# An attention-and-feed-forward kernel: seven products in place of eight in five output projections, and a planner with new costs

## The chip, the cores and the metric

The kernel runs on one core of a Trainium2 chip. The metric is the device time of one execution in microseconds (us). Before the change it is 1092.83 us, the median of three runs (1092.67 to 1093.36). A core has four engines that compute: PE (TensorE, matrix products), DVE (VectorE), ACT (ScalarE) and POOL (GpSimd). SP issues DMAs. Each engine works through its own instruction list in order and waits on semaphores for the others.

## The reference

Three stages follow each other, all in float32. Attention with a sigmoid in place of softmax, 4 batches, 12 heads, 448 positions, head size 64:

```python
scores = scale * np.matmul(q, k.transpose(0, 1, 3, 2)) - np.log(S)
attn = 1.0 / (1.0 + np.exp(-scores))
attn_out = np.matmul(attn, v)
```

Then a first feed-forward layer on the 1792 rows of width 768, and a second one with a gate:

```python
h = x @ w_in                          # 768 -> 2048
x = (h - np.tanh(h)) @ w_out          # 2048 -> 768
gate = 1.0 / (1.0 + np.exp(-(x @ w_gate)))   # 768 -> 1536
val = x @ w_val
out = (gate * val) @ w_out2           # 1536 -> 768
```

## The kernel before, in words

Products are made in float32 accuracy from operands that are split in two: a "high" part (ACT casts it) and a "low" part (DVE or POOL subtracts the high part). Each product is three matmuls, high by high, high by low and low by high, 448 columns wide. The four batches are the tiles t = 0 to 3.

*First layer.* For 32 steps i, `hidden_mm` computes a hidden block of 256 columns in 36 matmuls (`ph`, L399), ACT and DVE turn it into `g` by a chain of 12 operations (L433 to L472: squares, tanh, a polynomial, a predicated copy, then high and low of `g`), and a step of `po` matmuls (L506, 36 of them in six groups d = 0 to 5) projects it into `acc`. A group either adds `acc` on DVE (L519) or is seeded: ACT copies `acc` into the bank (L494), PE adds on top, ACT copies it back (L623). The last three steps are `tail_step`; the six groups of the very last step are put among the work of the second layer as "fillers".

*Second layer.* It runs in two passes over pairs of batches (`ps` 0 and 1), six blocks of 256 hidden columns each, so twelve blocks k = 0 to 11 (`block`, L1008). Both batches of a pair are multiplied together by seven products in place of eight (a 2 by 2 block scheme: operands `a11, a12, a22, s1 ... s4`, weights `b1, b22, t14, t32` mixed from four quarters). A product is nine matmuls (L1038). A block is seven products for the gate, n = 3k, and seven for the value, n = 3k+1, with the joins, copies and sigmoids between them, and ends with `gg`, high and low. The output projection of block k, n = 3k+2, stands in `groups2(k)`: for each of the two batches six groups of six matmuls (`pq`, L506), 72 in all. These groups are the fillers of block k+1: a plan `f{k}` of 14 numbers says how many groups stand behind each product.

*Operands.* `prepare` makes the x operands of a pass from `acc` (L667 sums, L801 high, L807 low). `divide` loads a block's 256 columns of weights (`mm`), mixes the quarters on DVE (L911, L916, L918), casts the high part on ACT (L881) and subtracts the low part on POOL or DVE (L892). Seven slots `w0` to `w6` hold them. `decoding` unpacks stored weights early (L181 to L199).

*What sets the order.* From step 28 of the first layer on, instructions are laid out by a planner in the kernel: `Task` objects with due times, `spend` which lets tasks start while PE works through a product, `must` for operations with a fixed place. It has a clock per engine (`busy`) and a clock `now` that follows PE's matmuls, with costs as constants in the code. Table `TUNE` shifts due times and chooses engines. The clock `now` grows by a fixed length per product:

```python
    def must(e, cost, f, ready=0.0):
        busy[e] = max(busy[e], now[0], ready) + cost
        f()
        return busy[e]
```

It does not stand still when PE must wait for a bank or an operand; only `force` moves it for an operation that has been left too late.

Of the kernel before, what the change touches and what calls it, by code (L numbers as in the profile page):

```python
# [64 lines left out]
}  # L65


@with_exitstack
def kernel(
# [462 lines left out]
    def groups1(i):  # L532

        at, gt, outs = outs1(i)
        for d in range(KD):
            def run(d=d):
# [4 lines left out]
                must("v", 0.65, lambda: sum_up(at, po, d, False, None))  # L541
# [66 lines left out]
    def tail_step(i, act, dve):  # L608
# [5 lines left out]
        def group(d):  # L614
            p = None
            if d % 2 and i > TAIL2:
                p = seeds.pop(d)
            p = project_group(f"po{i}_{d}", at, gt, outs, d, False, p, evict=False)
            if d % 2 == 0 and i > TAIL2:
                seeds[d + 1] = must("a", 0.55, lambda: None) and seed(f"po{i}_{d + 1}", at, d + 1)  # L620
            spend(1.2, TUNE.get("e4", 0.9), TUNE.get("e5", 1.0))
            if d % 2 and i > TAIL2:
                must("a", 0.55, lambda: nc.scalar.activation(  # L623
                    out=at[:, d], in_=p[:, :S], func=AF.Copy
                ))
# [12 lines left out]
        t4 = chain.add(dict(a=1.0), q2, [t2])
        td = chain.add(dict(v=1.1), d_, [t4])
# [42 lines left out]
    class Task:  # L682
# [11 lines left out]
        def start(self):  # L694
# [6 lines left out]
            if len(ways) > 1 and not self.haste and ways[1][0] < self.due - SPARE:  # L701
                return ways[1]
# [713 lines left out]
```

## Time and profile before

| | us |
|---|---|
| median of the runs | 1092.83 |
| the profiled execution | 1092.74 |
| its span (first to last instruction) | 1091.0 |
| PE busy in the span | 1078.5 (99%) |
| DVE, ACT, POOL busy | 822.6, 617.8, 384.9 |
| matmuls in the trace | 6085 |

The times of the rows come from the profiled execution; 1.74 us of it lie outside the span. A matmul here is a weight load that overlaps the matmul ahead, and the matmul itself. A mean duration of 362 ns in the page is that of one instruction in a pipeline; what a matmul takes out of the time is read from the chain of waits, which gives the start of each run of matmuls and their number. Line numbers are those of the kernel before.

### The profile page before, as it was taken

What the parts mean: (1) busy time and instruction counts of PE and PEld (TensorE: products, weight loads), DVE (VectorE), ACT (ScalarE), POOL (GpSimd) and SP (SyncE); (2) the same over time, 40 slices, a digit from 0 to 9 for tenths busy, and PEclk for the clock granted to TensorE, in tenths of its full rate; (3) what the DMA queues carried; (4) which work ended last, traced back from release to release, by engine and by line L of the source; (5) the groups of instructions that cost most, each with busy time, mean ns of one, the idle gap of its engine ahead of it and who ended that gap; (6) DMA issues with size and microseconds to landing.
All of it is one profiled execution on the core that took longest, in us unless ns stands there. A gap on an engine that the chain in (4) does not pass through costs nothing.

```text
span 1091.0 us, 15944 instructions
## 1 busy us (share of the span) xinstructions
PE 1078.5 (99%) x6085; PEld 971.6 (89%) x6085; DVE 822.6 (75%) x1153; ACT 617.8 (57%) x861; POOL 384.9 (35%) x391
## 2 busy tenths in 40 slices
PE   9999999999999999999999899999999999999998
PEld 5677789999999999999998799999999999999997
DVE  4778757899998989899978878898849664454344
ACT  6878845676777767777767545343454333333320
POOL 5455300011111110111126445565578524544621
PEclk9999999999999999999999999999999999999999
DMA  7676303334243434244320255454221411201202
GB/s 203 194 192 182 110 22 87 102 104 132 85 144 102 145 102 137 85 130 138 120 73 30 101 174 174 124 181 134 98 88 65 153 59 59 87 29 59 87 1 102
DMA packets 40204, 119.79 MB, mean 110 GB/s; under 512 B 6080, under 2 KB 21440, under 8 KB 40128
## 3 DMA queue, kind: packets, MB, share of 16 engines
q1 hardware_dynamic: 36896, 116.38, 33.2%
q0 software_dynamic: 3072, 2.17, 0.9%
q8 instruction: 48, 0.79, 0.3%
q10 hardware_dynamic: 160, 0.23, 0.1%
q14 instruction: 28, 0.23, 0.1%
HBM read 99.09 MB, written 19.66 MB: 109 GB/s over the span
## 4 chain that ended last, share of the span: by engine, by line
PE 96%; ACT 1%; DMA 1%; DVE 1%; POOL 0%; issue 0%; SPq 0%; ACTq 0%; DVEq 0%; POOLq 0%
PE ph L399 21%; PE po L506 21%; PE pq L506 16%; PE pa L1038 8%; PE pc L1038 8%; PE pb L1038 8%; PE pv L383 5%; PE pe L1038 4%; PE sa L346 4%; PE sl L358 1%; PE pv L376 1%; DMA st<-in_w_in_dram 0%; ACT at L350 0%; DMA kt<-in_k_dram 0%; POOL gg L1106 0%
## 5 line engine op out<-in xcount | busy, mean ns | idle before, releaser
L506 PE MATMUL po<-g,w 128*128 128x448 f32 x1152 | 238.9, 364 | 2.9 <-ACT g L469 2.7
L399 PE MATMUL ph<-x,w 128*128 128x448 f32 x1152 | 235.8, 362 | 0.2 <-ACT at L350 0.2
L506 PEld LDWEIGHTS po<-g,w 128*128 128x128 f32 x1152 | 215.2, 189 | 21.3 <-ACT g L469 3.0
L399 PEld LDWEIGHTS ph<-x,w 128*128 128x128 f32 x1152 | 215.8, 187 | 15.3 <-ACT at L350 0.6
L214 POOL TENSOR_TENSOR w<-m,w 128x384 fp32r<-128x384 f32 x64 | 63.6, 1016 | 376.5 <-issue 299.0
L506 PE MATMUL pq<-gg,w 128*128 128x448 f32 x864 | 184.3, 362 | 1.4 <-POOL gg L1106 0.8
L506 PEld LDWEIGHTS pq<-gg,w 128*128 128x128 f32 x864 | 161.8, 187 | 13.2 <-POOL gg L1106 1.5
L892 POOL TENSOR_TENSOR w_t<-mm,w_t 128x384 fp32r<-128x384 f32 x72 | 79.9, 1131 | 141.6 <-ACT w_t L881 137.8
L519 DVE TENSOR_TENSOR acco<-pq,acco 128x448 f32<-128x448 f32 x120 | 73.7, 621 | 72.9 <-PE pq L506 72.2
L1038 PE MATMUL pa<-a,w_b 128*128 128x448 f32 x432 | 94.2, 362 | 0.0
L1038 PEld LDWEIGHTS pa<-a,w_b 128*128 128x128 f32 x432 | 81.0, 187 | 5.4
L892 POOL TENSOR_TENSOR w_b<-mm,w_b 128x384 fp32r<-128x384 f32 x54 | 63.6, 1198 | 38.9 <-ACT w_b L881 36.7
L350 ACT ACTIVATE at<-sa,bias_s 128x896 f32<-128x896 f32 x72 | 67.3, 1006 | 8.1 <-PE sa L346 7.9
L436 ACT ACTIVATE y<-ph 128x896 f32<-128x896 f32 x32 | 29.4, 919 | 61.9 <-PE ph L399 61.9
L519 DVE TENSOR_TENSOR acc<-po,acc 128x448 f32<-128x448 f32 x90 | 55.4, 617 | 9.3 <-PE po L506 9.2
L181 ACT ACTIVATE m<-st 128x768 f32<-128x768 f32 x32 | 29.0, 907 | 56.6 <-POOL w L214 55.0
L383 PE MATMUL pv<-at,vt 128*64 128x224 f32 x576 | 59.8, 357 | 0.0
L383 PEld LDWEIGHTS pv<-at,vt 128*64 128x64 f32 x576 | 39.2, 137 | 18.9 <-issue 8.0
L346 PE MATMUL sa<-sp 64*128 64x448 f32 x432 | 50.8, 375 | 0.5 <-DVE sp L319 0.3
L1106 POOL TENSOR_TENSOR gg<-sg,gg 128x448 fp32r<-128x448 f32 x30 | 39.7, 1347 | 31.3 <-ACT gg L1101 31.1
L881 ACT ACTIVATE w_t<-mm 128x768 fp32r<-128x768 f32 x48 | 39.5, 838 | 19.9 <-DVE mm L918 14.1
L346 PEld LDWEIGHTS sa<-sp 64*128 64x128 f32 x432 | 38.5, 184 | 12.2 <-issue 7.3
(114 smaller groups left out, 1867.6 us busy)
## 6 DMA issues: line engine op xcount, KB each, us to landing
mm<-kept SPq DMA_DIRECT2D x36, 768.0 KB, 4.3
st<-in_w_out_dram SPq DMA_DIRECT2D x28, 768.0 KB, 4.9
st<-in_w_in_dram SPq DMA_DIRECT2D x16, 768.0 KB, 4.3
st<-in_w_gate_dram SPq DMA_DIRECT2D x12, 768.0 KB, 5.0
st<-in_w_val_dram SPq DMA_DIRECT2D x12, 768.0 KB, 4.9
kept<-mk SPq DMA_DIRECT2D x22, 384.0 KB, 5.5
kt<-in_k_dram SPq DMA_DIRECT2D x48, 112.0 KB, 3.5
kept<-mq SPq DMA_DIRECT2D x14, 384.0 KB, 5.6
```

The source lines that it names most:

```text
L214: (low or nc.gpsimd).tensor_tensor(out=w1[:, r], in0=mf[:, r], in1=w0[:, r].bitcast(F32), op=ALU.subtract)
L346: nc.tensor.matmul(pa[:, j, :S], kk[r, ki, c], qq[r, qi], start=(i == 0), stop=(i == 2),)
L350: nc.scalar.activation(out=at[:, :, c], in_=pa[:, :, :S], func=AF.Sigmoid, bias=bias_s, scale=qk_scale,)
L383: nc.tensor.matmul(po[j * D:(j + 1) * D, h, :SH], vt[:, j, c], at[:, j, c, h * SH:(h + 1) * SH], start=False, stop=(c == NCH - 2),)
L399: nc.tensor.matmul(o, w(i), xv(j), start=first and n == 0, stop=last and n == 2, skip_group_check=seeded,)
L436: nc.scalar.activation(out=y, in_=h, func=AF.Tanh)
L506: nc.tensor.matmul(po[:, :S], w[:, a, d], gt[:, c, j], start=n == 0 and not seeded, stop=n == last, skip_group_check=seeded,)
L519: nc.vector.tensor_tensor(out=at[:, d], in0=po[:, :S], in1=at[:, d], op=ALU.add)
L881: nc.scalar.activation(out=w0, in_=quarters(lo, hi), func=AF.Copy)
L892: eng.tensor_tensor(out=w1[:, r], in0=quarters(lo, hi)[:, r], in1=w0[:, r].bitcast(F32), op=ALU.subtract,)
L1038: nc.tensor.matmul(bank[term], w[:, i, half * KH + c], t[:, j, c], start=fresh and at == 0, stop=at == 3 * KH - 1, skip_group_check=not fresh,
L1106: eng.tensor_tensor(out=gt[t][:, 1, j], in0=sg[t][:, j], in1=gt[t][:, 0, j].bitcast(F32), op=ALU.subtract,)
```

## The change

In the second pass, five of the six output projections, those of blocks 6 to 10 (`wide(k)`), are computed by seven products in place of eight as well, now over both batches at once: 7 products by 3 column groups by 3 matmuls, 63 matmuls in place of 72. For this `divide` prepares the output weights of these blocks in the form that the other two matrices already have (four casts and four mixes in place of two casts, with an eighth slot and a half slot), `combine` mixes the block's result into the operands `t1` to `t4`, and `groups3` issues the products as eight fillers with their own banks (`a`, `b`, `c`, `e`), copies between banks on ACT, and 15 evictions on DVE in place of 12. What is common to both batches is gathered in a tile `accm`, and added once at the end (`shared`). Block 11 and the first pass keep `groups2`.

The planner gets new costs (smaller throughout), a clock `l` for operations of DVE and POOL that it holds to exclude each other, ready times for banks and operands (`until` moves `now` when PE is planned to wait), and a `lag` that due times are shifted by. All numbers of `TUNE` are new. The first block takes the product `a12` ahead of `s2` (`TERMS0`).

```diff
-    "f0": [0, 0, 4, 0, 0, 0, 2, 0, 0, 0, 0, 0, 0, 0],
+    "early": 3, "f0": [0, 0, 5, 0, 1, 0, 0, 0, 0, 0, 0, 0, 0, 0],
...
+    TERMS0 = ("a11", "s1", "a12", "s2", "s3", "s4", "a22")
...
     def must(e, cost, f, ready=0.0):
-        busy[e] = max(busy[e], now[0], ready) + cost
+        busy[e] = max(busy[e], now[0] + 0.2, ready) + cost
         f()
-        return busy[e]
+        return busy[e] + SHOW
+
+    def until(t, who=None):
+        if t > now[0]:
+            lag[0] += t - now[0]
+            now[0] = t
...
+            ways = []
+            for e, cost in kinds.items():
+                at = max(t, busy[e], busy["l"] if lock else 0.0)
+                ways.append((at + cost, at, e))
...
+    def wide(k):
+        return NBLK <= k < NK - 1
...
-        if kind == 2:
-            pair(0, 0, 2, [ld])
-            pair(1, 2, 4, [ld])
+        either = dict(v=0.485, g=0.93)
+        if wide(k) and kind == 2:
+            b22 = pair("b22", [3], [ld])
+            b1 = pair("b1", [0, 2], [ld])
+            t = task.add(either, mix(3, 1, 3, ALU.add), [b22])
+            t = task.add(either, mix(1, 0, 1, ALU.subtract), [t, b1])
+            pair("t14", [1, 3], [t])
+            t = task.add(either, mix(0, 3, 0, ALU.subtract), [t])
+            t = task.add(either, mix(2, 2, 0, ALU.subtract), [t])
+            pair("t32", [0, 2], [t])
...
+            operand("t1", 6.0, u1, lambda c: gt[1][:, c, 0], b12, b11)
+            operand("t2", 8.0, u2, lambda c: gt[2][:, 1, c], b22, u1, "t1")
+            operand("t3", 10.0, b12, lambda c: gt[2][:, 0, c], b22, b12, "t1")
+            operand("b22", 10.5, b22, lambda c: gt[1][:, c, 1])
+            operand("t4", 13.0, u4, lambda c: gt[2][:, 2, c], b21, u2, "t2")
...
+    PLAN_W = [0, 0, 1, 0] + [1] * 7 + [0] * 3
...
+        def pa_(d):
+            mm("p1", d, "a")
+            return lambda: copy("b", "a", d), 0.6
+
+        def pb_(d):
+            mm("p5", d, "e")
+            mm("p2", d, "a")
+            mm("p6", d, "b")
+
+            def then():
+                copy("c", "b", d)
+                evict(both, d, "e", d)
+                evict(left, d, "a", d)
...
+        def pc_(d):
+            mm("p7", d, "c")
+            mm("p3", d, "b")
...
+        def pd_(d):
+            mm("p4", d, "c")
...
+        return [
+            filler((pa_, 0)), filler((pb_, 0)), filler((pc_, 0), (pa_, 1)),
+            filler((pd_, 0), (pb_, 1)), filler((pc_, 1), (pa_, 2)), filler((pd_, 1), (pb_, 2)),
+            filler((pc_, 2)), filler((pd_, 2)),
+        ]
...
-            fillers = list(groups2(k))
+            fillers = groups3(k) if wide(k) else list(groups2(k))
```

How the change moves instructions is shown at three places. PE, where the last step of the first layer meets block 0 of the second (`pa`, `pe`, `pb` are banks of products, `po` the last step's groups, `g` the result of the last chain). Before:

```order
L506 MATMUL po_5_5764<-g_5581,w_5390 128x448
L1038 MATMUL pa_5789<-a_0_5569,w_b_5459 128x448 x9
L1038 MATMUL pe_5792<-s_0_5697,w_t_5648 128x448 x9
L1038 MATMUL pb_5790<-s_0_5822,w_t_5702 128x448 x9
L506 MATMUL po_0_5852<-g_5704,w_5266 128x448
L506 MATMUL po_0_5852<-g_5704,w_5390 128x448
```

And now:

```order
L515 MATMUL po_5_5758<-g_5579,w_5390 128x448
L1117 MATMUL pa_5787<-a_0_5693,w_b_5459 128x448 x9
L1117 MATMUL pe_5790<-s_0_5802,w_t_5531 128x448 x9
L1117 MATMUL pa_5787<-a_0_5576,w_b_5459 128x448 x9
L515 MATMUL po_0_5846<-g_5701,w_5266 128x448
L515 MATMUL po_0_5846<-g_5701,w_5390 128x448
```

The third product needs `a12`, which was made earlier, in place of `s2`; then five groups `po_0` to `po_4` follow where there were four.

DVE at the same place: the last chain's operations (on `ph` and `y`, ending with the low part of `g`), the operands `s` and `a` of pass 0, and sums into `acc`. Before:

```order
L456 SCALAR_TENSOR_TENSOR ph_5651<-s_5708,ph_5651 128x2x448
L193 SCALAR_TENSOR_TENSOR mq<-st_5346,mq 128x768
L199 SCALAR_TENSOR_TENSOR mq<-st_5346,mq 128x768
L807 TENSOR_TENSOR s_0_5822<-acc_1996,s_0_5822 128x448 x3
L461 SCALAR_TENSOR_TENSOR ph_5651<-s_5709,ph_5651 128x2x448
L466 COPY_PREDICATED y_5706<-mk_5707,ph_5651 128x896
L472 TENSOR_TENSOR g_5704<-y_5706,g_5704 128x896
L807 TENSOR_TENSOR a_0_5838<-acc_2110,a_0_5838 128x448
```

And now:

```order
L459 SCALAR_TENSOR_TENSOR ph_5652<-s_5705,ph_5652 128x2x448
L464 SCALAR_TENSOR_TENSOR ph_5652<-s_5706,ph_5652 128x2x448
L469 COPY_PREDICATED y_5703<-mk_5704,ph_5652 128x896
L836 TENSOR_TENSOR s_0_5802<-acc_2110,s_0_5802 128x448 x3
L475 TENSOR_TENSOR g_5701<-y_5703,g_5701 128x896
L836 TENSOR_TENSOR s_0_5819<-acc_1996,s_0_5819 128x448 x3
L684 TENSOR_TENSOR acc_2110<-acc_1996 128x448 x3
```

Two operations of `decoding` and the low part of `s2` no longer stand inside the chain; the low part of `s1` does, ahead of its last operation.

PE at the start of block 7, whose fillers are the first projection by seven products (`gg` are the block's results, `w` the output weights). Before:

```order
L1038 MATMUL pc_7763<-a_1_7724,w_t_7917 128x448 x9
L1038 MATMUL pa_8093<-a_1_7339,w_b_7941 128x448 x9
L1038 MATMUL pe_8096<-s_1_7553,w_t_7996 128x448 x9
L506 MATMUL pq_0_0_8129<-gg_0_7758,w_0_8054 128x448
L506 MATMUL pq_0_0_8129<-gg_0_7758,w_1_8069 128x448
```

And now:

```order
L1117 MATMUL pa_8098<-a_1_7472,w_b_7942 128x448 x9
L1117 MATMUL pe_8101<-s_1_7562,w_t_8006 128x448 x9
L1117 MATMUL pb_8099<-s_1_7632,w_t_8030 128x448 x9
L1357 MATMUL pq_a_8146<-gg_0_7746,w_b_8046 128x448 x3
L1117 MATMUL pa_8098<-a_1_7620,w_b_7942 128x448 x9
L1117 MATMUL pc_8100<-s_1_7832,w_t_8030 128x448 x9
L1357 MATMUL pq_e_8182<-gg_1_7747,w_t_8087 128x448 x3
L1357 MATMUL pq_a_8146<-gg_0_7746,w_b_8046 128x448 x3
L1357 MATMUL pq_b_8153<-gg_2_7748,w_t_8128 128x448 x3
```

A bank is now filled by three matmuls, and the first mixed operand (`gg_1` in `pq_e`) is wanted five products after the block before has ended, in place of all of `gg_0` after two.

## Rows read from the trace of the kernel before

**Rows 1.** The page's first part: busy us, share of the span, instructions.

```profile
PE 1078.5 (99%) x6085; PEld 971.6 (89%) x6085; DVE 822.6 (75%) x1153; ACT 617.8 (57%) x861; POOL 384.9 (35%) x391
```

**Rows 2.** Blocks 3, 10: length, busy PE PEld DVE ACT POOL, PEclk, DMA, GB/s.

```profile
714.16:753.76 39.60, 39.60 (x200) 37.12 (x199) 33.75 (x42) 16.76 (x26) 24.41 (x19) 1.00 0.48 150
...
991.36:1030.96 39.60, 39.60 (x200) 37.12 (x199) 17.40 (x28) 14.53 (x23) 21.63 (x21) 1.00 0.15 48
```

**Rows 3.** Chain that ended last, 572 to 641: start, us, what.

```profile
572.77 7.63 PE po L506 x36
580.39 7.20 PE ph L399 x36
...
595.39 1.80 PE pa L1038 x9
...
640.36 3.60 PE pq L506 x18
```

**Rows 4.** Timeline of PE there: start, us, what [idle before <-releaser].

```profile
600.83 2.21 PE L1038 MATMUL pb<-s,w_t 128*128 128x448 f32 x9 [1.84 <-ACT s L801]
605.77 6.97 PE L506 MATMUL po<-g,w 128*128 128x448 f32 x24 [2.73 <-ACT g L469]
```

**Rows 5.** Stretches of 2 us behind those waits, columns as rows 2.

```profile
606.00:608.00 2.00, 1.95 (x7) 1.47 (x7) 2.00 (x3) 1.75 (x2) 0.99 (x1) 0.72 0.08 9
608.00:610.00 2.00, 2.00 (x7) 1.80 (x6) 1.92 (x3) 0.00 (x0) 0.37 (x1) 0.50 0.85 316
```

**Rows 6.** Timelines of ACT, then of DVE, over the last chain.

```profile
593.32 0.54 ACT L494 ACTIVATE po<-acc 128x448 f32<-128x448 f32 x1
...
597.73 1.04 ACT L445 ACTIVATE s<-mk,gb 128x896 f32<-128x896 f32 x1
...
599.47 1.31 ACT L801 ACTIVATE s<-acc 128x1344 fp32r<-128x1344 f32 x1
...
604.76 0.95 ACT L469 ACTIVATE g<-y 128x896 fp32r<-128x896 f32 x1 [1.16 <-DVE y L466]
...
600.81 1.70 DVE L807 TENSOR_TENSOR s<-acc,s 128x448 fp32r<-128x448 f32 x3 [1.79 <-ACT s L801]
602.42 1.09 DVE L461 SCALAR_TENSOR_TENSOR ph<-s,ph 128x896 f32<-128x896 f32 x1
603.55 1.18 DVE L466 COPY_PREDICATED y<-mk,ph 128x896 f32<-128x896 int32 x1
605.75 1.09 DVE L472 TENSOR_TENSOR g<-y,g 128x896 fp32r<-128x896 f32 x1 [1.02 <-ACT g L469]
```

**Rows 7.** Timelines of PE, then ACT and POOL, at the end.

```profile
1071.13 1.08 PE L506 MATMUL pq<-gg,w 128*128 128x448 f32 x4 [0.56 <-ACT gg L1101]
1072.43 0.47 PE L506 MATMUL pq<-gg,w 128*128 128x448 f32 x1 [0.22 <-POOL gg L1106]
1073.52 13.68 PE L506 MATMUL pq<-gg,w 128*128 128x448 f32 x67 [0.62 <-POOL gg L1106]
...
1070.12 0.95 ACT L1101 ACTIVATE gg<-sg 128x896 fp32r<-128x896 f32 x1 [6.14 <-DVE sg L1070]
...
1071.22 4.47 POOL L1106 TENSOR_TENSOR gg<-sg,gg 128x448 fp32r<-128x448 f32 x4 [13.26 <-ACT gg L1101]
```

**Rows 8.** By line, operations of one kind: duration ns min/median/max, first and last start.

```profile
L892 POOL TENSOR_TENSOR w_t<-mm,w_t x72: 1008/1021/1746, 582.9 to 1044.8; 128x384 fp32r<-128x384 f32 x72
L892 DVE TENSOR_TENSOR w_t<-mm,w_t x24: 546/552/1041, 589.5 to 1046.2; 128x384 fp32r<-128x384 f32 x24
L1106 POOL TENSOR_TENSOR gg<-sg,gg x30: 1130/1158/1872, 676.6 to 1074.5; 128x448 fp32r<-128x448 f32 x30
L911 DVE TENSOR_TENSOR mm<-mm x24: 942/948/1908, 572.9 to 1039.1; 128x768 f32<-128x768 f32 x24
L916 DVE TENSOR_TENSOR mm<-mm x24: 541/557/1410, 576.2 to 1041.1; 128x384 f32<-128x384 f32 x24
L519 DVE TENSOR_TENSOR acco<-pq,acco x120: 605/625/625, 681.2 to 1087.2; 128x448 f32<-128x448 f32 x120
```

More of the change, by code (lines that the diff above doesn't have):

```diff
@@ L137 @@
     w_t = {}
-    w_free = list(range(7))
+    NW = 7
+    w_free = list(range(NW))
     def w_alloc(name, shape):
         n = w_free.pop(0)
-        return n, wp.tile(shape, F32R, tag=f"w{n}", name=name)
+        pool, tag = (stp, "st0") if n == NW else (wp, f"w{n}")
+        return n, pool.tile(shape, F32R, tag=tag, name=name)
     NU1 = 4 * G1
@@ L699, in start @@
             t = max([t, now[0]] + [self.end[i] for i in after])
-            ways = [(max(t, busy[e]) + cost, max(t, busy[e]), e) for e, cost in kinds.items()]
-            if len(ways) > 1 and not self.haste and ways[1][0] < self.due - SPARE:
+            ways = []
+            for e, cost in kinds.items():
+                at = max(t, busy[e], busy["l"] if lock else 0.0)
+                ways.append((at + cost, at, e))
+            if len(ways) > 1 and not self.haste and ways[1][0] < self.due + lag[0] - SPARE:
                 return ways[1]
@@ L716, in force @@
             self.go(self.start())
-            now[0] = max(now[0], self.end[-1])
+            until(self.end[-1], self.name)
         def flush(self):
@@ L939, in last @@
             over()
-        task.ops[-1] = (kinds, last, after, gate)
+        task.ops[-1] = (kinds, last, after, gate, lock)
     mq = []
@@ L1005 @@
     }
+    BANK = dict(a11="a", s1="e", s2="b", a12="a", s3="c", s4="b", a22="c")
     LAST = {"a12": "b1", "s3": "t32", "a22": "t14"}
@@ L1051, in product, with copy, sigmoid @@
                 half_free[n % 3] = now[0] + 0.3
-        def copy(out, src):
-            must("a", 0.55, lambda: nc.scalar.activation(out=out, in_=src, func=AF.Copy))
+        def copy(out, src, *banks):
+            t = must("a", 0.465, lambda: nc.scalar.activation(out=out, in_=src, func=AF.Copy),
+                     bank_t.get(banks[0], 0.0))
+            for c in banks:
+                bank_t[c] = max(t, bank_t.get(c, 0.0))
         late = {}
-        def sigmoid(out, src, ready=None):
+        def sigmoid(out, src, ready=None, bank=None):
             def f():
@@ L1137, in fill @@
                     fillers.pop(0)()
-        for at, term in enumerate(TERMS):
+        for at, term in enumerate(TERMS0 if k == 0 and TUNE.get("o0", True) else TERMS):
             product(3 * k, term)
@@ L1195, in groups2, with groups3, mm, copy @@
                 yield run
+    def groups3(k):
+        gt = g_t.pop(("b", k))
+        n = 3 * k + 2
+        first = k == NBLK
+        if first:
+            for b in (2, 3):
+                acc["o", b] = acc_tile(b, f"acco{b}")
+        left, right, both = acc["o", 2], acc["o", 3], acc["m"]
+        moving = dict(
+            b11=lambda c: gt[0][:, c, 0], b21=lambda c: gt[0][:, c, 1],
+            b22=lambda c: gt[1][:, c, 1], t1=lambda c: gt[1][:, c, 0],
+            t3=lambda c: gt[2][:, 0, c], t2=lambda c: gt[2][:, 1, c], t4=lambda c: gt[2][:, 2, c],
+        )
+        kinds = dict(
+            p1=("b1", 0, "b11"), p2=("b1", 1, "b21"), p3=("t32", 1, "b22"),
+            p4=("b22", 0, "t4"), p5=("t14", 1, "t1"), p6=("t32", 0, "t2"), p7=("t14", 0, "t3"),
+        )
+        bank = {}
+        def mm(p, d, c):
+            key, h, x = kinds[p]
+            require(n, key)
+            g = g_task[k, 0 if x in ("b11", "b21") else x]
+            g.finish()
+            until(max(g.end), g.name)
+            w, v = wk[n, key][1], moving[x]
+            fresh = p in ("p1", "p5")
+            until(bank_t.get("abce".index(c), 0.0))
+            if fresh:
+                bank[c, d] = pb_tile(f"pq{k}_{c}{d}", "abce".index(c))
+            for i, (a, b) in enumerate(((0, 0), (1, 0), (0, 1))):
+                nc.tensor.matmul(
+                    bank[c, d][:, :S], w[:, a, h * KH + d], v(b),
+                    start=fresh and i == 0, stop=i == 2, skip_group_check=not fresh,
+                )
+        def copy(c, o, d):
+            bank[c, d] = pb_tile(f"pq{k}_{c}{d}", "abce".index(c), True)
+            t = must("a", 0.465, lambda: nc.scalar.activation(
+                out=bank[c, d][:, :S], in_=bank[o, d][:, :S], func=AF.Copy
+            ), bank_t.get("abce".index(c), 0.0))
+            for at in (c, o):
+                at = "abce".index(at)
+                bank_t[at] = max(t, bank_t.get(at, 0.0))
+        def evict(at, col, c, d):
+            t = must("v", 0.55, lambda: sum_up(at, bank[c, d], col, first, None))
+            c = "abce".index(c)
+            bank_t[c] = max(t, bank_t.get(c, 0.0))
+        def pa_(d):
[9 more added lines that the diff above has]
+                evict(left, d, "a", d)
+                if d == KH - 1:
+                    w_free.append(wk[n, "b1"][0])
+            return then, 1.8
+        def pc_(d):
+            mm("p7", d, "c")
+            mm("p3", d, "b")
+            def then():
+                evict(right, KH + d, "c", d)
+                evict(right, d, "b", d)
+                if d == KH - 1:
+                    w_free.extend(wk[n, key][0] for key in ("t14", "t32"))
+            return then, 1.2
+        def pd_(d):
+            mm("p4", d, "c")
+            def then():
+                evict(left, KH + d, "c", d)
+                if d == KH - 1:
+                    half_free[2] = now[0] + 0.3
+            return then, 0.6
+        def filler(*parts):
+            def run():
+                thens = [f(d) for f, d in parts]
+                spend(sum(t for _, t in thens), TUNE.get("e10", 0.9), TUNE.get("e11", 0.3))
+                for f, _ in thens:
+                    f()
+            return run
+        return [
[3 more added lines that the diff above has]
+        ]
@@ L1197, with shared, f @@
+    def shared():
+        task = g_task["m"] = Task("m", now[0] - lag[0] + 6.0)
+        for h in range(2):
+            for d in range(KH):
+                def f(eng, at=acc["o", 3][:, h * KH + d], m=acc["m"][:, d]):
+                    eng.tensor_tensor(out=at, in0=at, in1=m, op=ALU.add)
+                task.add(dict(v=0.55, g=1.07), f)
     with tc.manual_schedule():
```

261 lines of the change are left out of this document (176 added, 85 removed), and 62 rows, old and new, of the table TUNE.

## The prediction

> **What bounds the kernel now.** I read the page's first part to see which engine is full, then busy time by block to see whether it ever stops, then the chain of waits and the timelines where it does. PE is busy for 1078.5 of the span's 1091.0 us [rows 1]; DVE, at 822.6, is next. From block 3 to block 10, eight stretches of 39.60 us, PE is busy for all 39.60 at full clock [rows 2]. A block is 126 matmuls of products and 72 of fillers, 198, so one matmul costs 39.60 / 198 = 0.200 us there, and nothing else in a block shows in the time. PE stops in two places of the part that the change touches. One is the hand-off from the first layer to the second. From 572.77 to 640.36, 67.59 us, it works through 297 matmuls (step 29 with 72, step 30 with 72, the last step's 36 `po`, and 117 of block 0's products) [rows 3]. At 0.200 these are 59.40, so 8.19 are lost. The other is the end, where `gg` of block 11 is awaited [rows 7].
>
> **Part A, the matmuls removed.** Blocks 6 to 10 project by 63 matmuls in place of 72: 5 x 9 x 0.200 = 9.0 us. This holds only as long as PE still never stops in blocks 7 to 11, where these groups are fillers.
>
> **Part B, the hand-off.** Here is where the 8.19 go. The `po` groups of step 29 take 7.63 where a step takes 7.20: 0.43. Those of step 30 run from 587.59 (580.39 + 7.20) to 595.39, 7.80: 0.60 [rows 3]. PE then waits 1.84 for the high part of `s2`, and 2.73 for the last chain's `g` [rows 4]. [...] The 24 `po` matmuls there take 6.97 where 4.80 are due [rows 4].
>
> What makes `g` late is seen in ACT and DVE [rows 6]. On ACT the second factor (L445, 1.04) starts at 597.73, since a copy out of the bank `po_5` and a copy of `pa`, both waiting for PE, stand ahead of it. On DVE the next operation of the chain, L461, stands behind three low parts of an operand, which wait for ACT's cast at 599.47, and runs only at 602.42.
>
> The change puts that second factor right behind the seed of the last group (the L494 row, 593.32 to 593.86), ahead of the copy out of `po_5`. I walk it with the durations there [rows 6]: factor 593.9 to 594.95, L461 and the predicated copy behind it (1.09 + 1.18, with 0.2 of hand-over) to 597.4, `g` high on ACT (0.95) to 598.4. DVE does the low parts of one operand (1.70) to 599.1, then `g` low (1.09) to 600.2. PE now has three products that need neither, `a11`, `s1` and `a12`, 27 x 0.200 = 5.4 from 595.4 on, and reaches `po_0` at 600.8 at the earliest, so `g` is there and PE does not stop for it. `s2`, which was late, is wanted only after five groups (30 matmuls, 6.0 us later). What I leave standing is 0.4 + 0.4 for the seeds of steps 29 and 30 (their order stays), 0.5 for the low parts of `s1`, which DVE ends at 599.1, while `pe` wants them from about 598.5 on, and 0.4 for one more late low part in the groups that follow: 1.7. [...] Gain: 8.2 - 1.7 = 6.5. Bounds: 0, if the waits are only moved, and 8.2. The two unpacking operations that leave this place on DVE go to earlier steps, where PE works through 36 matmuls of `ph` between groups and DVE has gaps; I cost them at nothing, and uncovered they would cost about the 1.09 of L461 each, as DVE operations of a like size.
>
> **Part C, the end.** Before, PE waits 0.56, 0.22 and 0.62 among its last matmuls: `gg` high ends on ACT at 1071.07, and the low parts come from POOL at 4.47 / 4 = 1.12 each [rows 7]. In the changed order a last group of three matmuls (0.6) stands between the last product and the first `pq`, which covers the 0.56, and the low parts are on DVE, at the 0.62 of a sum of the same shape [rows 8]. I leave 0.2 of the 1.40: gain 1.2, bounds 0 and 1.4. The six additions of `shared` stand under the 36 matmuls (7.2 us) of the first batch's groups and cost nothing; uncovered they would be 4 x 1.13 + 2 x 0.62 = 5.8 on two engines, at most 4.5 long. What follows the last matmul is as before. SP's DMAs are the same in number and size.
>
> **Part D, new waits.** Five blocks have more side work: 51 instructions more on DVE, 60 on ACT and 40 on POOL in all. By the order, a block from 7 on has about 42 DVE and 22 POOL instructions; at 0.55 to 0.95 and 1.02 to 1.16 [rows 8] that is 26.3 and 23.6 us, 49.9 together in 37.8, or 1.32 per us. Block 3 had 33.75 + 24.41 = 58.2 in 39.60, 1.47 per us, and PE did not stop [rows 2]. ACT goes from the 14.5 of block 10 to some 21. So there is room on average, and what can go wrong is order: PE now waits for a bank after every three matmuls, for operands `t1` to `t4` that DVE mixes, and for weights `t14`, of which the mix is a chain of seven operations on POOL and DVE. By row durations the banks and the operands come 1 to 2 us early, and `t14` of two value weights (blocks 8 and 11) 0.5 early. Nothing of before shows such a wait, so I bound it: nothing, or a wait of the size of the 1.84 row [rows 4] in each of the five, 9.2. I take 0.3 per block, 1.5, near the low end, because of the eight stretches without a stop. Another 0.2 for the start of block 7, where ACT's copy of a bank stands behind casts. The first pass has a new order with the same work: 0, with 0 and 2 as bounds, as block 3 has as much side work per us as any and no stop.
>
> **Sum.** -9.0 - 6.5 - 1.2 + 1.5 + 0.2 = -15.0. The profiled execution, 1092.74 (1091.0 of span and 1.74 around it), becomes 1077.74; it stands 0.09 under the median, so I forecast 1077.8.
>
> [...] The instructions that DVE and POOL both work on stretch at times [rows 8]: a low part on POOL from 1.01 to 1.75, a mix on DVE from 0.94 to 1.91 or 0.54 to 1.41. [...]
>
> **Rivals.**
> *Shared delays.* The chain of `t14` holds four low parts on POOL and three operations on DVE. Stretched each as far as rows 8 show (0.74 four times, 0.97, 0.87 and 0.50), it is 5.3 later; by half, 2.65. Less the 0.5 of slack, 2.15 in each of five blocks, 10.7 in place of the 1.5: 1077.8 + 9.2 = 1087.0. For it: the maxima of rows 8. Against it: the medians of the same rows lie 0.01 to 0.02 above the minima, so most instructions are not stretched, and block 3. Chance 0.17.
> *The hand-off wait is only moved*, say to `s1` or to a seed: B gains nothing, 1077.8 + 6.5 = 1084.3. For it: ACT has as many casts there as before. Against it: the walk above, with 0.6 or more left for `g`. Chance 0.09.
> *All waits go*, 9.0 + 8.2 + 1.4 gained and none new: 1092.8 - 18.6 = 1074.2. Chance 0.04.
> *Slower.* The chain of `t14` is stretched fully in every block, 5.3 - 0.5 = 4.8 each, 24, and the clock falls behind each such wait as it did at 606, about 2.0 (between the 1.56 that the two stretches of rows 5 lose and 6.97 - 4.80), another 10: 1077.8 - 1.5 + 34 = 1110. It decides once waits pass (15.0 + 1.5) / 5 = 3.3 us per block. For it: a stop of 1.84 has been followed by one of 2.73 and half clock. Against it: it needs every operation at its maximum. Chance 0.04.
>
> **How the numbers follow.** The forecast holds 0.66. Its own range is 1074.5 to 1081 (B down to 4.3 or D up to 4.7, and the other way all of B and C). The range to 1085.0 takes in the moved hand-off and leaves out most of the shared delays and the slower case; the low end is 1074.0. A difference of 0.2% (2.2 us, 1090.6 to 1095.0) is what a measurement can tell from none. Faster by more: 0.94, all cases but the slower one and the upper edge of the shared delays (0.02, within 0.2%); slower 0.04.
>
> **What would show it.** Right: 6040 matmuls in place of 6085 [rows 1]; blocks 7 to 10 at 37.8 us with PE busy throughout and a granted clock of 1.00; no wait over 0.5 for `g` and `s2` near 600, and a granted clock of 1.00 from 600 to 610; first `pq` of block 11 after less than 0.3. Wrong: PE waits at the products whose weights are `t14`, with DVE or POOL as releaser, or at the groups of three matmuls, for a copy or an eviction of their banks; low parts on POOL whose median, not only maximum, lies well over 1.02; a wait for `g` that has turned into one for `s1`. I would be wrong on the sum if the new waits in blocks 7 to 11 pass 5 us, or if the hand-off keeps more than half of its 8.2.

## The result and the profile after

The changed kernel takes 1081.71 us, the median of four runs (1081.54 to 1081.99), against 1092.78 before: a ratio of 0.9898, 95% interval 0.9881 to 0.9915. The forecast was 1077.8 with a range of 1074.0 to 1085.0. The direction and the three sources of gain were right, the size was 3.9 too large.

The page's first part after, columns as in [rows 1]:

```profile
PE 1070.5 (99%) x6040; PEld 961.7 (89%) x6040; DVE 851.0 (79%) x1204; ACT 647.1 (60%) x921; POOL 421.6 (39%) x431
```

The 45 matmuls are gone and PE is still the bound. The span fell from 1091.0 to 1079.9, by 11.1. To see where from, take every start of a matmul in the trace and add up what two neighbours are apart beyond 0.200 us (differences under 0.05 left out). That gives PE's loss by stretch; the losses of the other kernels below are taken in the same way:

| lost by PE, us | hand-off, 560 to 640 | first pass, blocks 1 to 5 | blocks 6 to 11 | end |
|---|---|---|---|---|
| before | 8.1 | 0.0 | 0.0 | 2.2 |
| after | 3.6 | 0.0 | 3.7 | 0.5 |

So 9.0 (matmuls) + 4.5 (hand-off) + 1.8 (end) - 3.7 (new waits) = 11.6. The step of 28 begins 0.35 later in this execution, in code that is the same, and the rest is rounding. PE's timeline at the hand-off, to set against [rows 3, 4]:

```profile
572.96 6.85 PE L515 MATMUL po<-g,w 128*128 128x448 f32 x30
580.03 1.48 PE L515 MATMUL po<-g,w 128*128 128x448 f32 x6 [0.22 <-ACT po L503]
581.35 7.36 PE L402 MATMUL ph<-x,w 128*128 128x448 f32 x36
...
595.14 1.47 PE L515 MATMUL po<-g,w 128*128 128x448 f32 x6 [0.22 <-ACT po L503]
596.46 1.97 PE L1117 MATMUL pa<-a,w_b 128*128 128x448 f32 x9
598.54 2.59 PE L1117 MATMUL pe<-s,w_t 128*128 128x448 f32 x9
600.96 1.97 PE L1117 MATMUL pa<-a,w_b 128*128 128x448 f32 x9
602.77 6.16 PE L515 MATMUL po<-g,w 128*128 128x448 f32 x30
608.77 1.96 PE L1117 MATMUL pb<-s,w_t 128*128 128x448 f32 x9
611.35 2.08 PE L1117 MATMUL pc<-s,w_t 128*128 128x448 f32 x9 [0.62 <-ACT pc L1133]
```

The waits of 1.84 and 2.73 are gone: 30 `po` matmuls take their 6.0 from 602.77 to 608.77. From 600 to 610 the granted clock is 1.00, where it had been 0.72 and 0.50 in the last four of these us [rows 5]. What is left, 3.6 in all, stands at four places. Step 29's groups take 581.35 - 572.96 = 8.39 for 7.20: 0.5 at the last group, whose seed stands on ACT behind the chain's first factor, 0.4 where the low part of `g` of the chain before ends late on DVE, the rest at the seed of a group before. Step 30 loses 0.7 at its seeds. The product of `s1` (`pe`) loses 0.9, ahead of its start and at its low parts. And from 608.77 to 611.35 stand 2.58 for 1.80, 0.9 with the edge behind: ACT's copy from bank b to c starts at 610.77, when the product of `s2` has ended (608.77 + 1.96), and no group stands behind that product:

```profile
610.77 0.53 ACT L1133 ACTIVATE pc<-pb 128x448 f32<-128x448 f32 x1 [1.43 <-PE pb L1117]
```

Blocks 6 to 11, columns as in [rows 2]:

```profile
828.66:869.23 40.57, 40.45 (x200) 36.91 (x198) 31.10 (x50) 15.41 (x25) 22.80 (x20) 1.00 0.33 113
869.23:908.21 38.98, 38.35 (x190) 35.30 (x189) 30.40 (x45) 19.60 (x34) 25.12 (x23) 1.00 0.22 77
908.21:946.41 38.20, 38.08 (x191) 35.38 (x189) 30.52 (x45) 20.65 (x35) 22.96 (x22) 1.00 0.18 63
946.41:984.43 38.02, 38.02 (x190) 35.37 (x189) 28.00 (x42) 19.58 (x34) 25.01 (x22) 1.00 0.12 42
984.43:1023.18 38.75, 38.09 (x190) 35.39 (x189) 29.43 (x45) 19.97 (x34) 24.99 (x23) 1.00 0.24 82
1023.18:1060.98 37.80, 37.80 (x190) 35.26 (x188) 25.29 (x39) 18.26 (x31) 21.63 (x20) 1.00 0.07 22
```

Block 6 has 1.0 over its 39.60, the next four 1.2, 0.4, 0.2 and 0.95 over 37.80; block 11 has nothing (it issues 186 matmuls up to there, 37.2, and 0.6 of its projection). How one of these waits comes about is seen in block 10, on PE, ACT, DVE and POOL in turn:

```profile
1014.07 0.88 PE L1357 MATMUL pq_c<-gg,w_t 128*128 128x448 f32 x3 [0.67 <-ACT pq_c L1364]
...
1013.49 0.53 ACT L1364 ACTIVATE pq_c<-pq_b 128x448 f32<-128x448 f32 x1 [3.65 <-PE pb L1117]
...
1009.03 1.76 DVE L966 TENSOR_TENSOR mm<-mm 128x768 f32<-128x768 f32 x1 [1.57 <-POOL w_b L939]
1011.70 0.56 DVE L971 TENSOR_TENSOR mm<-mm 128x384 f32<-128x384 f32 x1 [0.91 <-POOL w_b L939]
1012.30 0.56 DVE L973 TENSOR_TENSOR mm<-mm 128x384 f32<-128x384 f32 x1
1012.77 0.62 DVE L528 TENSOR_TENSOR acco<-pq_c,acco 128x448 f32<-128x448 f32 x1
...
1007.97 3.70 POOL L939 TENSOR_TENSOR w_b<-mm,w_b 128x384 fp32r<-128x384 f32 x3
```

Read it from below (`w_b` on POOL are low parts of weights): three of them take 3.70 and not 3 x 1.02; beside them a mix on DVE takes 1.76 and not 0.95, and the next mix waits 0.91 more for POOL. The eviction of bank `pq_c` stands behind these mixes on DVE, so it starts at 1012.77; ACT's copy into the bank waits for it (the view names PE, whose last matmuls into `pq_b` began at 1010.84 and took 0.76), and PE for ACT. Such waits for evictions behind mixes are three of the losses: 0.40 in block 7, 0.22 in block 9, 0.94 in block 10, together 1.56. The wait at the start of block 7, 0.79, has another place in a queue. On ACT the bank copy L1133 stands behind the cast of `t14`, which waited for mixes on POOL, and behind a cast of `gg`:

```profile
873.50 2.07 PE L1117 MATMUL pb<-s,w_t 128*128 128x448 f32 x9 [0.51 <-ACT pb L1133]
...
871.71 0.85 ACT L925 ACTIVATE w_t<-mm 128x768 fp32r<-128x768 f32 x1 [1.80 <-POOL mm L957]
872.46 0.56 ACT L1216 ACTIVATE gg<-sg 128x448 fp32r<-128x448 f32 x1
872.93 0.53 ACT L1133 ACTIVATE pb<-pa 128x448 f32<-128x448 f32 x1
...
869.28 2.39 POOL L957 TENSOR_TENSOR mm<-mm 128x384 f32<-128x384 f32 x2
```

Block 6 loses 1.0, 0.66 of it where PE waits for low parts of `gg` on DVE, and block 8 loses 0.39, where the last two groups of block 7's projection stand side by side. At the end, the row that answers to [rows 7]:

```profile
1060.38 0.77 PE L1357 MATMUL pq_c<-gg,w_b 128*128 128x448 f32 x3
1061.11 14.90 PE L515 MATMUL pq<-gg,w 128*128 128x448 f32 x72
```

The three matmuls of the new last group cover `gg` high, and 72 matmuls follow in 14.90 with 0.5 lost.

### The profile page after: what moved, and what is told of

Its sections match the earlier page's. It is cut to its first block, busy times and chain, and to the rows that moved or that the text cites. A ratio compares the mean times of both kernels' runs of the same rounds, so it can differ in the third digit from the quotient of the medians.

```text
span 1079.9 us, 16056 instructions
## 1 busy us (share of the span) xinstructions
PE 1070.5 (99%) x6040; PEld 961.7 (89%) x6040; DVE 851.0 (79%) x1204; ACT 647.1 (60%) x921; POOL 421.6 (39%) x431
## 4 chain that ended last, share of the span: by engine, by line
PE 87%; issue 4%; POOL 3%; DVE 3%; ACT 2%; DMA 1%; SPq 0%; DVEq 0%; POOLq 0%; ACTq 0%
PE ph L402 20%; PE po L515 19%; PE pq L515 8%; PE pc L1117 7%; PE pb L1117 7%; PE pa L1117 7%; PE pv L386 5%; PE sa L349 4%; PE pe L1117 3%; POOL w_b L939 2%; PE pq_c L1357 1%; PE pq_a L1357 1%; PE pq_b L1357 1%; PE sl L361 1%; PE pv L379 1%
## 5 line engine op out<-in xcount | busy, mean ns | idle before, releaser
L939 POOL TENSOR_TENSOR w_t<-mm,w_t 128x384 fp32r<-128x384 f32 x104 | 110.4, 1087 | 88.5 <-ACT w_t L925 82.0
L939 POOL TENSOR_TENSOR w_b<-mm,w_b 128x384 fp32r<-128x384 f32 x81 | 95.4, 1201 | 35.5 <-ACT w_b L925 34.5
L515 PE MATMUL pq<-gg,w 128*128 128x448 f32 x504 | 107.5, 363 | 0.1
L515 PEld LDWEIGHTS pq<-gg,w 128*128 128x128 f32 x504 | 94.4, 188 | 7.6 <-DVE gg L1191 1.1
L925 ACT ACTIVATE w_t<-mm 128x768 fp32r<-128x768 f32 x58 | 47.9, 842 | 47.4 <-DVE mm L973 25.0
L528 DVE TENSOR_TENSOR acc<-po,acc 128x448 f32<-128x448 f32 x90 | 55.6, 618 | 14.7 <-PE po L515 14.6
L528 DVE TENSOR_TENSOR acco<-pq,acco 128x448 f32<-128x448 f32 x72 | 43.9, 619 | 28.1 <-PE pq L515 27.9
L925 ACT ACTIVATE w_b<-mm 128x768 fp32r<-128x768 f32 (+1 forms) x58 | 38.5, 675 | 18.2 <-PE pq_c L1357 8.4
```

The lines of the kernel that those rows point to most:

```text
L515: nc.tensor.matmul(po[:, :S], w[:, a, d], gt[:, c, j], start=n == 0 and not seeded, stop=n == last, skip_group_check=seeded,)
L528: nc.vector.tensor_tensor(out=at[:, d], in0=po[:, :S], in1=at[:, d], op=ALU.add)
L925: nc.scalar.activation(out=w0, in_=src, func=AF.Copy)
L939: eng.tensor_tensor(out=w1, in0=quarter(i), in1=w0.bitcast(F32), op=ALU.subtract)
```

## The experiments

In all but the first, the order of instructions is held: a copy of the planner's own decisions is laid down as a table, and entries are moved. An entry such as `w33/7/v` is operation 7 of the weights n = 33 on DVE (a is ACT, g is POOL); the row's name is the stretch of PE's work in which it starts, `31s2` the product `s2` of n = 31, `pq9_d1_b2` a group of block 9's projection. The table reproduces each engine's list but for what an edit moves. Lines in these kernels count 7 to 16 higher behind the planner. Beside these runs the kernel before took 1092.9 to 1093.2, against 1092.8 beside the changed kernel, so differences of up to 0.4 to the changed kernel's 1081.71 are not read as effects.

**Planner alone.**

```diff
     def wide(k):
-        return NBLK <= k < NK - 1
+        return False
```

> The changed kernel with the planner, costs and TUNE as they are, but no block wide: all output projections by eight products as before (72 matmuls), with the five old filler plans for blocks 7 to 11. Theory: the five narrow projections are worth 45 x 0.200 = 9.0 us of PE, less the 2.7 us of new waits that the changed kernel has in blocks 7 to 11, so this kernel takes 1081.7 + 9.0 - 2.7 = 1088.0, and the gain of 4.8 against the kernel before is all from the hand-off near 600 us and the end. Rival: the new costs give no gain of their own, and this one stands within 2 us of 1092.8; or they are worth more without the wide blocks, under 1086.

1088.17 (1087.84 to 1088.39), ratio 0.9952 (0.9940 to 0.9965). The loss is 3.4 at the hand-off, 1.0 in block 6, none in blocks 7 to 11, 1.1 at the end. So the five narrow projections are worth 1088.2 - 1081.7 = 6.5: 9.0 of matmuls less the waits that they bring. The other 4.6 come from the planner, with `a12` ahead of `s2` in block 0. The rivals are out.

**The factor moved up in the kernel before.**

```diff
-po30_5: c30/5/a xs4_0/0/g xs4_0/1/v
-0a11: c30/6/v xs4_0/2/g
-0s1: c30/7/a d22/2/v d22/3/v
+po30_5: c30/5/a xs4_0/0/g xs4_0/1/v c30/6/v c30/7/a
+0a11: xs4_0/2/g c30/8/v c30/9/v
+0s1: c30/10/a c30/11/v
```

> The kernel before, instruction order held as it was, but for the last chain of the first layer: the second factor (L445) goes right behind the first, ahead of the copies that wait for PE, the two unpacking operations leave the chain, and g high and low go ahead of the s2 operand. The product order stays a11, s1, s2. Theory: the wait of 3.0 us for g goes, the one of 2.0 us for s2 stays, and if the slow clock behind it comes from both waits together most of the 1.9 us goes too: 1092.8 - 3.0 = 1089.8, down to 1087.9. Rival (g is late for another reason, or s2 gets later by as much): 1092 to 1093.

1094.84 (1094.19 to 1097.70), ratio 1.0017 (1.0008 to 1.0026): a miss. `g` is in time, but with its high part ahead of it PE loses 3.44 at `s2`, 1.4 more than before (the view has 3.27 of it as the wait), and the granted clock is at 0.50 from 602 to 608. The wait has moved by one operand; 2.3 more are lost from 615 to 620, at the products of `s4` and `a22`.

**And `a12` ahead of `s2`**, in three versions, each with what the one before had shown:

```diff
-        for at, term in enumerate(TERMS):
+        for at, term in enumerate(TERMS if k else TERMS0):
```

> As the one with the second factor moved, and in block 0 the product a12 ahead of s2, with the four groups of the last step ahead of s2 too; s2's operand is made right behind g. Theory: neither s2 nor g is waited for, the granted clock stays at 1.00, and this holds the changed kernel's whole gain at the hand-off (4.5) or more, as two seeds' waits are smaller here: 1092.8 - 4.5 to -6.5 = 1086.3 to 1088.3. Rival (the gain there comes from the planner's many other moves): not below 1089.

1095.02 (1093.64 to 1096.30): a miss. `s2` and `g` are in time, as the theory has it: 0.4 lost from 595 to 602. The next link then pays for all of them, and half clock follows from 612 to 619. PE's waits in this kernel (us, times, longest):

```profile
PE pc L1050 <- ACT pc L1067: 5.9, 1, 5.9
```

ACT's copy stood behind the cast of `s3`, and that behind sums on DVE that came late, behind the two unpacking operations that I had put there (1.91 and 1.77 long).

> The kernel before, instruction order held, with the second factor and g moved up and a12 ahead of s2, as measured at 1095.0, where s2 and g were in time but a copy for s3 waited 5.9 behind sums that DVE had not reached. Now the two unpacking operations stand in step 30, the sums for s4 and s3 come right behind s2's low parts, and the last two groups stand between s2 and s3. Theory (the hand-off is one chain of ACT and DVE from the factor to s3, and pays only when no link is late): s3's wait goes, the clock stays up, 1087 to 1089. Rival (the gain of the changed kernel there needs more than order, so another wait comes): 1091 or more.

1093.32 (1092.11 to 1095.49), no change: a miss. (In this version and the next, four and three operations have also gone from POOL to DVE.) Now the unpacking in step 30 took 1.90 and 1.80, `g` was late by 2.3 again, and 2.0 were lost at `a22`.

> The kernel before, instruction order held, with the second factor and g moved up, a12 and four groups ahead of s2, two groups between s2 and s3, the sums for s4 and s3 right behind s2's low parts, and the two unpacking operations of the last step not in step 30 (where they took 1.90 and 1.80 us and delayed g) but in block 1, with the later unpackings shifted in the same way. Theory (the hand-off's gain is this order alone: no DVE operation that is not on the chain stands in it): s2, g and s3 are in time, at most 3 us are lost from 572 to 640 where 8.2 were, and the time is 1087 to 1089. Rival (unpacking later, or mixing of block 0's weights, makes a new wait in blocks 0 to 3, or s3 is still late): 1090.5 or more.

1094.92 (1093.68 to 1096.74), a miss as well. The hand-off's loss is 5.5 in place of 8.1, with `s2`, `g` and `s3` in time, `s4` 2.2 late and `a22` 1.2; but 2.6 are lost in block 2, where nothing had been lost. The unpackings were moved into blocks 0 to 2 (n = 1 to 6). 1.5 of the 2.6 stand behind one of them on ACT (L181 at 678.14, which waited 2.05 for a DMA); for the other 1.1 the cause was not followed. Gain and loss weigh each other out. The profiled execution (1096.37) also reaches the first layer 3.6 later than the kernel before, ahead of everything that was moved, with a granted clock of 0.50 from 31.7 to 35.1, so its time is not that of the moves alone. In the kernel before I did not get the gain by hand, and it stays open how few moves would give it.

**The other way round: two parts undone in the changed kernel.** The unpacking goes back into the chain:

```diff
-0a11: c30/8/v c30/9/v xs1_0/3/a xs1_0/4/v
+0a11: d22/2/v d22/3/v c30/8/v c30/9/v xs1_0/3/a xs1_0/4/v
```

> The changed kernel, instruction order held, but for two DVE instructions: the two unpacking operations that stood inside the last chain before are put back between its third and fourth DVE operation. Theory (each DVE instruction in that chain delays s1's low parts, g and the sums one for one): s1's product is reached 1.9 to 2.4 later, and if the wait brings the half clock as it did before, 1.9 more: 1083.6 to 1086. Rival (DVE has room there, and another link sets the pace): under 1082.5.

1086.31 (1085.15 to 1087.05), ratio 0.9931 (0.9917 to 0.9944): 4.6 slower than the changed kernel. DVE, PE, then stretches of 2 us (length, busy PE, PEclk, DMA, GB/s):

```profile
597.09 1.83 DVE L196 SCALAR_TENSOR_TENSOR mq<-st,mq 128x768 int32<-128x768 int32 x1
598.95 0.96 DVE L202 SCALAR_TENSOR_TENSOR mq<-st,mq 128x768 int32<-128x768 int32 x1
```

```profile
602.65 1.81 PE L1128 MATMUL pe<-s,w_t 128*128 128x448 f32 x3 [2.05 <-DVE s L847]
604.26 3.29 PE L1128 MATMUL pa<-a,w_b 128*128 128x448 f32 x9
```

```profile
602.00:604.00 2.00, 1.22 (x3) 0.92 0.88 280
604.00:606.00 2.00, 2.00 (x6) 0.50 0.77 221
606.00:608.00 2.00, 2.00 (x8) 0.73 0.84 319
```

Two instructions, 2.8 us on DVE, bring a wait of 2.05 for the low parts of `s1`, and behind it the clock goes to 0.50: the nine matmuls of `pa` take 3.29. The factor goes back instead:

```diff
-po30_5: c30/6/a c30/7/v
-0a11: c30/8/v c30/9/v xs1_0/3/a xs1_0/4/v
-0s1: c30/10/a c30/11/v xs2_0/3/a xs2_0/4/v
+0a11: xs1_0/3/a xs1_0/4/v
+0s1: c30/6/a c30/7/v c30/8/v c30/9/v c30/10/a c30/11/v xs2_0/3/a xs2_0/4/v
```

> The changed kernel, instruction order held, but the second factor of the last chain goes back behind the copies out of po_5 and pa that wait for PE, and the chain's later operations with it, behind s1's low parts. Theory (the place of this factor makes g late): g high comes at 604.1 in place of 600.0, PE, which reaches po_0 at 602.2 as s1 is now earlier, waits 1.9, and with the half clock loses up to 1.9 more: 1083.1 to 1085.0. Rival (three products ahead of po_0 cover it): 1081.2 to 1082.0.

1086.09 (1085.46 to 1086.43), ratio 0.9932 (0.9919 to 0.9944): 4.4 slower, more than expected. PE:

```profile
605.00 6.61 PE L515 MATMUL po<-g,w 128*128 128x448 f32 x30 [2.09 <-ACT g L472]
...
614.52 2.08 PE L1128 MATMUL pc<-s,w_t 128*128 128x448 f32 x9 [1.10 <-ACT pc L1145]
```

The granted clock is 1.00 here in each stretch of 2 us from 602 to 610; but the sums for `s3` are late in turn, and PE pays 1.3 at `pc` and 0.8 further on. By the traces the hand-off loses 4.1 more in the one kernel and 4.2 in the other: either part undone takes nearly the whole 4.5, so the gain at the hand-off needs both. Two other parts of the change there, `a12` ahead of `s2` and the fifth group, were not undone.

**The mixes behind the evictions.**

```diff
...
-pq9_d1_b2: w33/5/g w33/6/v w33/7/v w33/8/v
+pq9_d1_b2: w33/5/g w33/6/v
...
+31s2: w33/7/v w33/8/v
```

> The changed kernel, instruction order held, but for six DVE instructions: in blocks 7, 9 and 10 the last two mixes of the next weights (L971, L973) stand behind the three evictions of the projection's banks rather than ahead of them. Theory (the waits at 898.6, 975.0 and 1013.0 are DVE's queue: a mix that waits for a low part on POOL holds the eviction, which holds ACT's bank copy, which holds PE): the 0.40 + 0.22 + 0.94 = 1.56 us go, 1080.1. Rival (the copies are late on ACT, or the weights get late in turn): 1081.3 or more.

1080.06 (1079.96 to 1080.89), ratio 0.9880 (0.9866 to 0.9893), as the theory said. In block 10 the mix is still stretched, but the evictions follow it at once, and PE has no wait there:

```profile
1008.43 1.76 DVE L977 TENSOR_TENSOR mm<-mm 128x768 f32<-128x768 f32 x1 [1.56 <-POOL w_b L950]
1010.12 0.61 DVE L528 TENSOR_TENSOR acco<-pq_c,acco 128x448 f32<-128x448 f32 x1
...
1011.71 0.54 DVE L982 TENSOR_TENSOR mm<-mm 128x384 f32<-128x384 f32 x1
```

**POOL that only writes.**

```diff
-                    eng.tensor_tensor(
-                        out=w1, in0=quarter(i), in1=w0.bitcast(F32), op=ALU.subtract
-                    )
+                    if eng is nc.gpsimd and n > 18:
+                        eng.memset(w1.bitcast(F32), 0.0)
+                    else:
...
```

> The changed kernel, instruction order held, with POOL's weight low parts from block 6's value weights on replaced by a fill with zeros, which reads nothing (those low parts are left out of the result). Theory (DVE operations with two operands in SBUF and POOL operations that read SBUF hold each other up): from 870 us on L966 takes 0.95 each time, where its median was 1.47, L957 0.55 with no 1.37, and the waits at 898.6, 975.0 and 1013.0 go, also as the mixes no longer wait for POOL: 1080 or a little under. Rival (the stretch comes from PE's or the DMA's reads): L966 stays at a median over 1.3.

1079.09 in one run, with a span of 1076.8 in place of 1079.9. By line from 840 us on, ns minimum, median and maximum, first and last start: the mixes, the evictions from bank `pq_c` and POOL's low parts of the changed kernel, then the mixes and POOL's fill here:

```profile
L966 DVE TENSOR_TENSOR mm<-mm x11: 947/1474/1758, 848.3 to 1037.8; 128x768 f32<-128x768 f32 x11
...
L528 DVE TENSOR_TENSOR acco<-pq_c,acco x24: 616/624/626, 922.5 to 1062.2; 128x448 f32<-128x448 f32 x24
...
L939 POOL TENSOR_TENSOR w_b<-mm,w_b x46: 998/1028/1833, 839.1 to 1035.3; 128x384 fp32r<-128x384 f32 x46
```

```profile
L980 DVE TENSOR_TENSOR mm<-mm x11: 948/949/952, 847.0 to 1034.5; 128x768 f32<-128x768 f32 x11
...
L951 POOL MEMSET w_t<- x57: 411/418/425, 840.5 to 1028.6; 128x384 f32 x57
```

With nothing read by POOL's low parts, the mix of two operands in SBUF takes 0.95 all eleven times, four of them with POOL's fills running beside it. In the changed kernel the lengthening has a pattern, here in block 10:

```profile
1008.94 1.03 POOL L939 TENSOR_TENSOR w_b<-mm,w_b 128x384 fp32r<-128x384 f32 x1
1009.03 1.76 DVE L966 TENSOR_TENSOR mm<-mm 128x768 f32<-128x768 f32 x1 [1.57 <-POOL w_b L939]
1009.92 1.75 POOL L939 TENSOR_TENSOR w_b<-mm,w_b 128x384 fp32r<-128x384 f32 x1
```

The low part that began first takes its usual time and ends at 1009.97; the mix ends 0.82 after it, and the low part that began during the mix ends 0.88 after the mix. Of the eleven mixes (L966) from 840 us on, eight are like this one and end 0.82 after the low part that they began behind; eight low parts that began during a mix end 0.87 to 0.88 after it. Once the two began within 0.01 of each other, and the low part was the one held, 1.83 long. So one of the two ended nearly its own usual length (0.95 or 1.02) behind the other, as if held for it, and apart from that one case it was the one that began second. DVE's operations with an operand in a bank (L526, L528 and L1152, 145 from 840 us on) took 0.61 to 0.63 each, 100 of them with POOL at work beside them; with the fill the means of these lines are 0.62 to 0.63 as well. Of the 3.7 lost in blocks 6 to 11, 0.4 remain, the one wait that is no matter of DVE and POOL (the last two groups of block 7's projection side by side). The fill is also shorter than a low part, 0.42 for 1.02, so what speaks for the stretch are the durations of the mixes; the waits go for both reasons.

**The group behind `s2`.**

```diff
-    "f0": [0, 0, 5, 0, 1, 0, 0,
+    "f0": [0, 0, 4, 1, 1, 0, 0,
...
-po31_4: xs3_0/3/a xs4_0/5/g
-0s2: xs3_0/4/v xs3_0/5/v xs3_0/6/v w1/2/v
+po31_4: xs4_0/5/g
+0s2: xs3_0/3/a xs3_0/4/v xs3_0/5/v xs3_0/6/v w1/2/v
```

> The changed kernel, instruction order held, but in block 0 four groups of the last step behind a12 and one behind s2, in place of five and none; ACT's cast for s3 moves with it. Theory (the 0.89 at 610.4 is ACT's copy from bank b to c, which starts when s2's product ends and which nothing covers): a group of 1.2 us behind s2 covers it, 1081.7 - 0.9 = 1080.8. Rival (s2 or s3 get late by the same amount): 1081.5 or more.

1082.01 (1081.55 to 1082.94): a miss. The 0.9 at 610 are gone and 0.8 stand at 616, where the product of `a22` now comes earlier than its low parts.

**All local edits.** The six together, and then, after their traces, those that had not just moved a wait:

> The changed kernel, instruction order held, with six local edits: the mixes behind the evictions (measured alone at 1080.06), the group behind s2, a weight cast and a gg cast behind the bank copy at the start of block 7 (0.79), the last two groups of block 7's projection no longer next to each other in block 8 (0.39), the sixth group of steps 29 and 30 without a seed, added by DVE (1.0), two low parts of a22 of the second pass behind gg's in block 6 (0.66). Theory (each of these waits is one of queue order, and goes without another in its place): 1080.06 - 0.9 - 0.8 - 0.4 - 1.0 - 0.7 = 1076.3. Rival (half of them only move): 1078.2 or more.

1079.61 (1079.44 to 1079.86): the rival. Without step 30's seed `s1` lost 1.3 at 598.8, the group behind `s2` moved its wait, and new ones came at 863 and 948.

```diff
-18s3: xa22_1/2/v xa22_1/3/v g5_1/1/v w19/2/g
+18s3: g5_1/1/v w19/2/g
+pq5_1_0: xa22_1/2/v xa22_1/3/v
...
-19a22: g6_0/0/a w20/8/a
+19a22: g6_0/0/a
+21s1: w20/8/a w20/9/v w20/10/v g6b22/0/a
```

> The changed kernel, instruction order held, with local edits only: the mixes behind the evictions in blocks 7, 9 and 10 (1080.06 alone), two low parts of a22 behind gg's in block 6 (0.66, seen to go), the casts at the start of blocks 7 and 9 and two casts in block 6 behind the bank copies that PE waits for (0.79 and 0.07), and the sixth group of step 29 without a seed (0.5, seen to go; step 30 keeps its seed, without which s1's low parts came 0.9 late). Theory (each wait is one place in a queue): 1080.06 - 0.66 - 0.86 - 0.5 = 1078.0. Rival (as before, half of the gain turns into new waits): 1079.0 or more.

1078.08 (1077.78 to 1078.46), ratio 0.9862 (0.9848 to 0.9875): it beats both kernels, by 3.6 the changed one. It loses 2.9 at the hand-off and 1.0 in blocks 6 to 11. The kernel has one edit more than was written down for it: the last two groups of block 7's projection stand apart, as in the six together, and the 0.39 there is gone. With it the theory's 1078.0 would be 1077.6; waits of 0.3 and 0.4 for bank copies, at 862 and 876, are new.

## Why the prediction was right, and where it was off

The number lies in the stated range, but above the 1074.5 to 1081 that the prediction gave for its own case: the range held because it was drawn wide enough for a moved hand-off, which is not what happened.

*A, the matmuls* (9.0): right. The planner alone at 1088.2, with 2.7 of waits that only the wide blocks bring, leaves 6.5 + 2.7 = 9.2; against it the wide blocks save 0.6 at the end.

*B, the hand-off* (6.5, measured 4.5): right in its mechanism, wrong in what I left standing. I allowed 1.7 and 3.6 were lost. In the 8.2 stood 1.9 behind the two waits, where matmuls begin up to 0.54 apart in place of 0.200 (606.48 to 610.04), at granted clocks of 0.72 and 0.50 [rows 5]; the changed kernel loses nothing from 601 to 610, at 1.00. Step 29 costs 1.2 and not 0.4, the late low part of `g` and the seed behind the chain's factor on ACT; step 30 costs 0.7 for 0.4, and `s1` 0.9 for 0.5. The copy from bank b to c behind `s2`, 0.9, was not in my walk at all, because I followed operands there and no banks; in its place stood 0.4 for a late low part. One sentence was plainly wrong: the two unpacking operations do not go to earlier steps but to block 0's value products (at 624.3 and 630.3), and I costed them at nothing, or at 1.09 each. Put back, they take 1.83 and 0.96 and cost 4.6 in all, through the wait of 2.05 and the granted clock of 0.50 behind it.

*C, the end* (1.2, measured 1.8): right in its mechanism, and over its own bound of 1.4. The 1.4 are the waits that the view names; by the starts of the matmuls 2.2 were lost there. The planner alone leaves 1.1 of them, the changed kernel with its new last group 0.5.

*D, the new waits* (1.7, measured 3.7): the step that failed. The forecast's 0.3 per block was an average without a place, and its kind of wait, for a bank or for `t14`, was not followed through the queues. The stretch that the rival of shared delays reckons with was there, but at another place: PE never waited for `t14` itself. In blocks 7, 9 and 10 the lengthened mixes held up the evictions behind them on DVE, and through ACT's copies PE's next group of three; these 1.56 went when the mixes were put behind the evictions. I could have asked ahead of time, for each mix, what is queued behind it and not only who reads its result. The start of block 7, where I had seen the copy behind casts and taken 0.2, cost 0.79, with the late cast of `t14` in that queue. The 1.0 in block 6 and the 0.39 in block 8 were in no term; the planner alone has the 1.0 too, so it is no wait of the wide blocks. A sign of being wrong that the prediction named, waits at the groups of three for a copy or an eviction, thus came true, and blocks 7 to 10 are not at 37.8. The rival's price, 9.2 above the forecast, was far too high: not every chain meets a low part on POOL, and each wait is what the stretch leaves after the bank's own slack, 0.2 to 0.9 where I took 2.15. Of the stretch itself the runs show this: the mix of two SBUF operands on DVE took a median of 1.47 for 0.95 beside POOL's low parts, which read SBUF, and 0.95 each time with POOL's fills, which only write.

The two misses add up: -2.0 at B, -2.0 at D, +0.6 at C and -0.5 for the 0.35 ahead of step 28 and rounding, the 3.9 by which the forecast was too low.

## What to carry to other kernels

Where PE is full, cut matmuls, but walk every bank as well as every operand, and for each instruction that may be late ask what stands behind it on its engine. At a hand-off a wait that is removed shows the next link; here either of two moves undone took nearly all of the gain, and four tries by hand gave none of it. Where DVE mixes two SBUF operands while POOL subtracts from SBUF, as here, cost the mix with the rest of the POOL operation that it may meet (0.95 became up to 1.76 in this kernel), and put evictions ahead of it, which was worth 1.6 here.

## What was not expected of the hardware

Waits of about equal length were followed by different clocks. In the kernel with the unpacking back, PE waited 2.05 and the granted clock fell to 0.50 behind it; in the one with the factor back it waited 2.09 and the clock stayed at 1.00; in the kernel before it waited 1.84 with 1.00 behind it (600.8 to 602.6), and the 0.50 came only behind the second wait, of 2.73 [rows 4, 5]. Of the versions made by hand, the second has half clock from 620.5 on, behind a wait of 1.76, and the third has none behind one of 2.04. Behind the wait of 2.05 the next 12 matmuls took 4.74 (602.65 to 607.39) where 2.40 are due, behind the one of 2.09 the next 30 took 6.45 (605.00 to 611.45) where 6.00 are. What sets the clock behind such a wait the traces here do not settle.
